# Chunk-selecting attention with a squared-ReLU way up and down: earlier first scores, the first x in pairs, the last tokens in column halves, and some squares on GpSimd

## The chip, the cores and the metric

The kernel runs on one core of one Trainium2 chip. The metric is the device time of one execution in microseconds (us). The text calls the engines by the names of the profile: PE is TensorE (matrix products), DVE is VectorE, ACT is ScalarE, POOL is GpSimd, and SP is SyncE, which here only issues DMAs.

## The reference

Two stages follow one another. The first is attention over 4 batches, 8 heads, 768 tokens and 64 columns a head, in which each token looks only at the six key chunks (of 32 keys) that an upper bound picks. The second takes the result as 3072 tokens of 512 columns through a way up to 2048 columns, a ReLU, a square, and a way down.

```python
k_chunks = k.reshape(B, H, nc, chunk, D)              # chunk = 32, nc = 24
k_min, k_max = np.min(k_chunks, axis=3), np.max(k_chunks, axis=3)
ub = np.sum(np.maximum(q[:, :, :, None, :] * k_min[:, :, None, :, :],
                       q[:, :, :, None, :] * k_max[:, :, None, :, :]), axis=-1)
ub = np.where(causal, ub, -1e9)
top_chunks = np.argsort(ub, axis=-1)[..., -6:]
scores = scale * np.matmul(q, k.transpose(0, 1, 3, 2))
mask = sel & (pos[:, None] >= pos[None, :])           # sel: the token's six chunks
attn = softmax(np.where(mask, scores, -1e9))
x = np.matmul(attn, v)                                # to [3072, 512]
h = np.maximum(x @ w_in, 0.0)
out = h * h @ w_out
```

## The kernel before

The work is cut into eight half batches of 384 tokens (`ORDER`), and each of these into four pairs of heads, so there are 32 steps s (`slots`), which the text calls pairs 0 to 31. The order of all instructions is written by hand: each engine runs its own in the order in which the program lists them, and waits at the head of its queue for what an instruction needs.

A step has these parts. `step_P` transposes k and q of a pair on PE (tiles tk and tq); ACT makes the two ReLU parts of q (`relus_T`, tile qr) and DVE the chunk extrema (`extrema`, tiles km and kbd). `step_U` multiplies them into the upper bounds (ub), from which DVE takes the sixth largest (MAX8) and writes a comparison. `step_V` transposes that comparison (qt), and DVE copies it into kq, beside the q and k that `place` puts there. `step_E` multiplies the scores (ps), ACT takes the exponential (e), and POOL masks the diagonal blocks in place (an affine select on line 416). `step_F` multiplies e with v (po), and DVE divides into x. In the text the masks, po and x are counted by the pair.

When the four pairs of a half batch are done, `step_X` transposes x to xT; for half batches 0, 1 and 7 this runs on PE with a copy on DVE and one on ACT, for the others as a DMA. `ffn_up` is one of 16 column groups f of the way up: four products (ph), the ReLU on ACT (ht, line 491), and the square on DVE (h, line 493). `ffn_down` is one quarter of the way down for 128 tokens (py, line 503); after the fourth quarter the result is copied (ob) and stored. Both lie in a queue of pieces (`queue`), from which `f1` takes one at a time at chosen places of the next half batch's steps, so the way up of half batch 0 runs in pairs 4 to 7, four groups a pair, and its way down begins with pair 8.

The first two pairs' q and k come as float32 through SP's and ACT's queues (`load_staged`) and are cast (`step_cast`). Everything else is loaded by POOL's queue, at places that `at` and `go` give by the step. `busy(n)` multiplies n blocks of an identity into a tile that nobody reads. `blank` zeroes the columns of qn0 that carry the comparison for pairs 0 to 3; three memsets zero `nsel`, which does the same for later pairs. After the last step, `step_X(7)` and the whole way up and down of half batch 7 remain.

Of the kernel before, what the change touches and what calls it, by code (L numbers as in the profile page):

```python
# [16 lines left out]
HT = 3  # L17
# [22 lines left out]
def kernel(  # L40
# [231 lines left out]

    def place(s, n, copy):
        b, half, p = slots[s]
        for h in range(2):
            copy(by_token(kqs[b % 2][QROW[h]:QROW[h] + D, h, p, 2 * half + "kq".index(n), :]),  # L276
                 in_order(st[s][n][D * h:D * h + D]))
# [171 lines left out]
    h2 = {}  # L449

    def step_X(hb, pe):
        x = xs.pop(hb)
        xT = late.tile([128, NKI, HB], BF16, tag="xT", name="xT")
        if pe:
            for g in range(2):
                pt = psA.tile([128, 2, HB], BF16, tag="att", name="pt")
                for u in range(2):
                    for j in range(HT):
                        nc.tensor.matmul(
                            pt[:, u, 128 * j:128 * (j + 1)],  # L460
                            lhsT=x[:, j, 128 * (2 * g + u):128 * (2 * g + u + 1)],
                            rhs=ident, is_transpose=True, start=True, stop=True)
                if g:
                    nc.scalar.copy(xT[:, 2:4, :], pt)
                else:
                    nc.vector.tensor_copy(xT[:, 0:2, :], pt)
        else:
            for j in range(HT):
                nc.sync.dma_start_transpose(
                    out=xT[:, :, 128 * j:128 * (j + 1)], in_=x[:, j, :])  # L470
# [4 lines left out]
        downs.extend(ffn_downs(hb, hb == 2 * B - 1))  # L475
        if hb < 2 * B - 1:
            queue.extend(downs.pop(0) for _ in range(LAG))

    def ffn_downs(hb, tail=False):
        py = {}  # L480
        return [lambda act, t=t, c=c: ffn_down(hb, py, t, c, act, tail)
                for t in range(HT) for c in range(4)]

    def ffn_up(hb, xT, f):
# [7 lines left out]
        h = late.tile([128, HB], BF16, tag="h", bufs=2 * NFI + 2, name="h")  # L492
        nc.vector.tensor_mul(h, ht, ht)  # L493
        h2[hb, f] = h
# [81 lines left out]

    def busy(n):

        idle = psA.tile([128, 128], F32, tag="att", name="idle")
# [12 lines left out]
    place(0, "k", nc.scalar.copy)  # L592
    step_U(0)
    busy(9)
    step_cast("k", 1)
    step_cast("q", 1)
    for i in range(3):
        nc.vector.memset(nsel[i], 0.0)
    step_V(0)
    step_P(1)  # L600
    step_T2(1)
    for s in range(NP):
        step_E(s, 0, 0)
        step_E(s, 0, 1)
        step_E(s, 1, 0)
        busy(8)
        step_U(s + 1)
        if s + 1 < NP:
            place(s + 1, "k", nc.scalar.copy)
        else:  # L610
            place(s + 1, "k", nc.vector.tensor_copy)
        step_E(s, 1, 1)
        if s + 1 == NP:
            place(s + 1, "q", nc.scalar.copy)
        if s:
            step_F(s - 1, 0)
            step_F(s - 1, 1)
        step_V(s + 1)
        step_P(s + 2)
        if s + 1 < NP:  # L620
            relus_T(s + 2)
            extrema(st[s + 2]["k"], s + 2)
        go(s, 99)
# [6 lines left out]
    for s, (b, half, p) in enumerate(slots):  # L630
# [16 lines left out]
        if s == NP:  # L647
# [4 lines left out]
            relus_T(s + 1)  # L652
            early.close()
            late = ctx.enter_context(tc.tile_pool(name="late", bufs=2))
            step_X(0, True)
            extrema(st[s + 1]["k"], s + 1)
            place(s + 1, "k", nc.vector.tensor_copy)
            place(s + 1, "q", nc.scalar.copy)
        if s == 2 * NP:
            for n in range(hf):  # L660
                step_E(s, 0, n)
            relus_T(s + 1)
            place(s + 1, "q", nc.scalar.copy)
            step_F(s - 1, 0)
            step_F(s - 1, 1)
            f1()
            f1()
            step_X(1, True)
            extrema(st[s + 1]["k"], s + 1)
# [12 lines left out]
        if p == 0 and hb > 2:  # L682
            f1()
            f1()
        if hb > 1:
            f1()
# [37 lines left out]
    while queue:  # L724
        fill(1, len(queue) % 2 == 0)


# [28 lines left out]
```

## Time and profile before

| | |
|---|---|
| median of 3 runs | 281.27 us (281.25 to 281.73) |
| profiled execution | 281.18 us, of it span 279.5 us |
| PE busy | 261.1 us (93% of the span) |
| DVE busy | 169.0 us (60%) |
| ACT busy | 181.1 us (65%) |
| POOL busy | 91.9 us (33%), DMA issues counted |
| mean granted clock of PE | 0.986 |
| chain that ended last | PE 70%, DVE 13%, ACT 10%, issue 3%, DMA 2% |

The span is the time from the first to the last instruction of the profiled execution; its own time has 1.7 us more around it. A busy PE is not PE at its peak, as products are pipelined and their ends modelled. The chain that ended last is followed back from the last instruction, at each step to what released it. In a timeline each line gives the start, the busy time, the engine, the line of the program, the operation, and what it writes and reads; in brackets stands how long the engine was idle before it, and what ended that.

### The profile page before, as it was taken

How to read it: one execution, taken by the hardware profiler on the slowest of the kernel's cores; microseconds unless marked ns; L12 is line 12 of the kernel's file. 1: busy time of each engine (PE TensorE's matmuls, PEld its weight loads, DVE VectorE, ACT ScalarE, POOL GpSimd, SP SyncE). 2: the span in 40 equal slices, each digit the busy share in tenths (PEclk: the TensorE clock that was granted, in tenths of full speed). 3: DMA queues.
4: the chain of work that ended last, by engine and by line, in shares of the span. 5: the costliest groups of instructions: out<-in, count | busy, mean ns of one | idle time of the engine just before them, and what ended most of it. 6: DMA issues, size and time to landing. Idle time of an engine off the chain costs nothing.

```text
span 279.5 us, 6636 instructions
## 1 busy us (share of the span) xinstructions
PE 261.1 (93%) x2463; PEld 162.3 (58%) x2463; DVE 169.0 (60%) x643; ACT 181.1 (65%) x396; POOL 91.9 (33%) x137
## 2 busy tenths in 40 slices
PE   7686989899999999999999999999999999999994
PEld 7465556546657566665565566655565566755541
DVE  6688599656896248744795368635884355413411
ACT  6595699658986578845674687835674777715500
POOL 8696336513652104731452016521111111100000
PEclk9998699999999999999999999999999999999999
DMA  8999999957999547999599359996512200101101
GB/s 144 143 211 207 179 217 193 104 68 101 166 166 162 106 96 129 137 144 159 104 143 151 77 119 153 128 138 164 135 39 55 79 2 0 40 38 39 40 38 75
DMA packets 97840, 32.05 MB, mean 115 GB/s; under 512 B 84592, under 2 KB 93424, under 8 KB 97808
## 3 DMA queue, kind: packets, MB, share of 16 engines
q0 software_dynamic: 64720, 14.42, 62.7%
q1 hardware_dynamic: 32688, 17.11, 28.1%
q8 instruction: 19, 0.31, 0.5%
q10 hardware_dynamic: 400, 0.10, 0.2%
q14 instruction: 13, 0.11, 0.1%
HBM read 27.26 MB, written 6.29 MB: 120 GB/s over the span
## 4 chain that ended last, share of the span: by engine, by line
PE 70%; DVE 13%; ACT 10%; issue 3%; DMA 2%; SPq 1%; POOL 0%; ACTq 0%; POOLq 0%
PE py L503 28%; PE ph L487 23%; PE ps L407 9%; PE po L432 6%; ACT e L412 4%; DMA stage<-in_q_dram 2%; DVE h L493 2%; ACT ht L491 2%; DVE km L319 2%; DVE x L442 2%; ACT ob L509 1%; ACT qr L271 1%; ACT kq L276 1%; PE ub L354 1%; DVE kq L276 1%
## 5 line engine op out<-in xcount | busy, mean ns | idle before, releaser
L412 ACT ACTIVATE e<-ps 128x512 bf16<-128x512 f32 x192 | 96.7, 551 | 27.2 <-PE ps L407 27.1
L487 PE MATMUL ph<-xT,w_in 128*128 128x384 bf16 x512 | 101.9, 331 | 1.3 <-ACT ht L491 0.8
L503 PE MATMUL py<-w_out,h 128*128 128x512 bf16 x384 | 92.1, 379 | 1.8 <-ACT ob L509 1.6
L491 ACT ACTIVATE ht<-ph 128x384 bf16<-128x384 f32 x128 | 62.6, 499 | 27.8 <-PE ph L487 26.0
L416 POOL TENSOR_SCALAR_AFFINE_SELECT e<-e 128x384 bf16<-128x384 bf16 x64 | 34.3, 542 | 139.7 <-ACT e L412 138.5
L493 DVE TENSOR_TENSOR h<-ht 128x384 bf16<-128x384 bf16 x128 | 46.6, 375 | 45.6 <-ACT ht L491 45.3
L487 PEld LDWEIGHTS <-w_in 128*128 128x128 bf16 x512 | 48.3, 99 | 32.3 <-issue 5.2
L407 PE MATMUL ps<-kq 128*128 128x384 bf16 (+2 forms) x320 | 56.4, 278 | 2.5 <-DVE kq L393 1.8
L503 PEld LDWEIGHTS <-h 128*128 128x128 bf16 x384 | 36.4, 98 | 37.9 <-issue 2.5
L407 PEld LDWEIGHTS <-kq 128*128 128x128 bf16 x320 | 26.5, 98 | 15.3 <-issue 3.3
L361 DVE MAX8 m<-ub 128x8 f32<-128x24 f32 (+1 forms) x160 | 16.8, 172 | 22.4 <-PE ub L354 21.5
L432 PEld LDWEIGHTS <-e 128*128 128x128 bf16 x672 | 25.5, 98 | 5.6 <-POOL e L416 1.0
L432 PE MATMUL po<-vn,e 128*128 128x65 bf16 x672 | 26.9, 194 | 0.8 <-POOL e L416 0.8
L509 ACT COPY ob<-py 128x512 f32<-128x512 f32 x19 | 11.1, 585 | 22.7 <-PE py L503 22.3
L442 DVE TENSOR_TENSOR x<-po,r 128x384 bf16<-128x384 f32 x32 | 17.8, 558 | 1.1
L393 DVE COPY kq<-qt 64x384 bf16<-64x384 bf16 (+1 forms) x28 | 8.8, 315 | 12.2 <-PE qt L389 12.2
L105 POOL DMA_DIRECT2D kn<-in_k_dram x15 | 13.3, 888 | 0.2
L105 POOL DMA_DIRECT2D qn<-in_q_dram x15 | 13.3, 886 | 0.0
L319 DVE TENSOR_TENSOR km<-km 128x384 bf16<-128x384 bf16 (+3 forms) x40 | 11.5, 287 | 1.1
L354 PE MATMUL ub<-kbd,qr 128*128 128x48 bf16 (+1 forms) x160 | 9.3, 180 | 2.3 <-DVE kbd L218 1.1
L121 POOL DMA_DIRECT2D vn<-in_v_dram x12 | 10.7, 904 | 1.8 <-DVE kq L383 1.3
L511 DVE COPY ob<-py 128x512 f32<-128x512 f32 x5 | 3.5, 691 | 11.5 <-PE py L503 11.5
(63 smaller groups left out, 194.5 us busy)
## 6 DMA issues: line engine op xcount, KB each, us to landing
out_dram<-ob SPq DMA_DIRECT2D x24, 256.0 KB, 2.1
kq<-kqT SPq DMA_DIRECT2D x10, 384.0 KB, 4.9
w_in<-in_moe_w_in_dram POOLq DMA_DIRECT2D x2, 1024.0 KB, 13.0
w_out<-in_moe_w_out_dram POOLq DMA_DIRECT2D x2, 1024.0 KB, 18.8
kn<-in_k_dram POOLq DMA_DIRECT2D x15, 128.0 KB, 5.6
qn<-in_q_dram POOLq DMA_DIRECT2D x15, 128.0 KB, 5.5
vn<-in_v_dram POOLq DMA_DIRECT2D x12, 128.0 KB, 8.0
vn<-in_v_dram POOLq DMA_DIRECT2D x4, 384.0 KB, 7.1
```

Source lines behind the costliest of these rows:

```text
L105: nc.gpsimd.dma_start(out=nat_of(n, g)[:, DM * j:DM * j + DM].rearrange("p (h d) -> p h d", d=D), in_=rows(n, *ORDER[g], 0, H)[:, 128 * j: ...
L319: nc.vector.tensor_tensor(y, x[:, :, :, 0:m], x[:, :, :, m:2 * m], op=op)
L361: nc.vector.max(out=m8[:, j, hh, :], in_=ub[:, j - j0, hh, :])
L407: nc.tensor.matmul(ps[:, at:at + 128 * m], lhsT=kqs[b % 2][:, hh, p, 2 * (j // HT), 128 * (j % HT):128 * (j % HT + 1)], rhs=qc(s, hh)[:, c ...
L412: nc.scalar.activation(e[:, 512 * n + lo:512 * n + hi], ps[:, lo:hi], ACT.Exp, scale=float(scale))
L416: nc.gpsimd.affine_select(out=d, in_=d, compare_op=ALU.is_ge, fill=0.0, base=0, channel_multiplier=-1, pattern=[[0, 3], [1, 128]])
L432: nc.tensor.matmul(po[:, hh, i, :], lhsT=t["e"][hh][:, c:c + 128], rhs=vn[b % 2][:, 2 * p + hh, j, :], start=(j == 0), stop=(j == iq))
L442: nc.vector.tensor_mul(x[:, :, 128 * p:128 * (p + 1)].rearrange("p j (h d) -> p h j d", h=2), po[:, :, :, 0:D], r.to_broadcast([128, 2, HT ...
L487: nc.tensor.matmul(ph[:, 0:HB], lhsT=w_in[:, ki, 128 * f:128 * (f + 1)], rhs=xT[:, ki, :], start=(ki == 0), stop=(ki == NKI - 1))
L491: nc.scalar.activation(ht, ph[:, 0:HB], ACT.Relu)
L493: nc.vector.tensor_mul(h, ht, ht)
L503: nc.tensor.matmul(py[t], lhsT=h2[hb, f][:, 128 * t:128 * (t + 1)], rhs=w_out[:, f, :], start=(f == 0), stop=(f == NFI - 1))
```

## The change

Five things change, and a few names with them.

1. *Start.* One half of pair 1's staged q is issued from ACT's queue. The zeroing of qn0 goes from ACT to two memsets on POOL, ahead of POOL's first loads; the zeroing of nsel goes from DVE to ACT. The first two score products and exps of pair 0 are moved ahead of the cast of pair 1's q and of pair 1's transposes.
2. *First x.* The transposes of half batch 0 are cut: those of pairs 0 and 1 come while pair 3 is worked on, that of pair 2 after po of pair 3, and that of pair 3 alone at the end; the copies are all on DVE, and the PSUM space is that of the way up. Ten and eight identity products are put between. Half of the copy of k for pair 4 goes from DVE to ACT.
3. *Second x.* The transposes of pairs 4 and 5 are moved ahead of po of pair 7; one group of the way down is moved from before the third and fourth score products of pair 8 to later in it.
4. *Squares.* Of the 16 squares of half batch 0, the eight with odd f are computed on POOL.
5. *End.* The last 128 tokens go down in two halves of 256 columns; each is copied in two parts, on DVE and ACT, and stored by two DMAs, from SP's and ACT's queues.

```diff
-    load_staged("q", 1, nc.sync, nc.sync)
+    load_staged("q", 1, nc.scalar, nc.sync)
...
     make_identity(nc, ident)
+    for c in (0, 3):
+        nc.gpsimd.memset(qn0[:, :, :, c, :], 0.0)
     load_packed("k", 0, 4)
...
-    def blank():
-        for c in (0, 3):
-            nc.scalar.mul(qn0[:, :, :, c, :].rearrange("p j a d -> p (j a) d"),
-                          ident[:, 0:D].unsqueeze(1).to_broadcast([128, HT * NP, D]), 0.0)
+    def blank(i):
+        nc.scalar.mul(nsel[i].rearrange("p j h d -> p (j h) d"),
+                      ident[:, 0:D].unsqueeze(1).to_broadcast([128, 2 * HT, D]), 0.0)
...
+    def x_T(hb, g, pt, us=(0, 1)):
+        if (hb, g) not in pts:
+            pts[hb, g] = pt[0].tile([128, 2, HB], BF16, tag=pt[1], name="pt")
+        for u in us:
+            for j in range(HT):
+                nc.tensor.matmul(
+                    pts[hb, g][:, u, 128 * j:128 * (j + 1)],
+                    lhsT=xs[hb][:, j, 128 * (2 * g + u):128 * (2 * g + u + 1)],
+                    rhs=ident, is_transpose=True, start=True, stop=True)
+    def x_copy(hb, g, u0, u1, copy):
+        copy(xT_of(hb)[:, 2 * g + u0:2 * g + u1, :], pts[hb, g][:, u0:u1, :])
...
+    def ffn_last(hb):
+        t, w = HT - 1, DM // 2
+        r0 = S * ORDER[hb][0] + HB * ORDER[hb][1] + 128 * t
+        for g in range(2):
+            y = psS.tile([128, DM], F32, tag="ps", name="py")
+            for f in range(NFI):
+                nc.tensor.matmul(
+                    y[:, 0:w], lhsT=h2[hb, f][:, 128 * t:128 * (t + 1)],
+                    rhs=w_out[:, f, w * g:w * g + w], start=(f == 0), stop=(f == NFI - 1))
+            ob = late.tile([128, DM], F32, tag="ob", bufs=3, name="ob")
+            for c in range(2):
+                (nc.scalar.copy if c else nc.vector.tensor_copy)(
+                    ob[:, 128 * c:128 * c + 128], y[:, 128 * c:128 * c + 128])
+                (nc.scalar if c else nc.sync).dma_start(
+                    out[r0:r0 + 128, w * g + 128 * c:w * g + 128 * c + 128],
+                    ob[:, 128 * c:128 * c + 128])
...
-        nc.vector.tensor_mul(h, ht, ht)
+        (nc.gpsimd if hb == 0 and f % 2 else nc.vector).tensor_mul(h, ht, ht)
...
     busy(28)
-    blank()
     step_cast("k", 0)
+    blank(1)
     step_cast("q", 0)
+    blank(2)
...
     place(0, "k", nc.scalar.copy)
+    blank(0)
     step_U(0)
     busy(9)
     step_cast("k", 1)
+    step_V(0)
+    step_E(0, 0, 0)
+    step_E(0, 0, 1)
     step_cast("q", 1)
-    for i in range(3):
-        nc.vector.memset(nsel[i], 0.0)
-    step_V(0)
     step_P(1)
     step_T2(1)
+    early.close()
+    late = ctx.enter_context(tc.tile_pool(name="late", bufs=2))
     for s in range(NP):
-        step_E(s, 0, 0)
-        step_E(s, 0, 1)
+        last = s + 1 == NP
+        if s:
+            step_E(s, 0, 0)
+            step_E(s, 0, 1)
...
+        if last:
+            x_T(0, 0, F)
         step_V(s + 1)
         step_P(s + 2)
-        if s + 1 < NP:
+        if last:
+            x_copy(0, 0, 0, 2, nc.vector.tensor_copy)
+            busy(10, *F)
+        else:
...
             relus_T(s + 1)
-            step_X(0, True)
+            x_T(0, 1, F, (0,))
+            x_copy(0, 1, 0, 1, nc.vector.tensor_copy)
+            busy(8, *A)
+            x_T(0, 1, F, (1,))
+            x_copy(0, 1, 1, 2, nc.vector.tensor_copy)
+            push(0)
...
             place(s + 1, "q", nc.scalar.copy)
+            x_T(1, 0, A)
+            x_copy(1, 0, 0, 2, nc.vector.tensor_copy)
             step_F(s - 1, 0)
             step_F(s - 1, 1)
             f1()
             f1()
-            step_X(1, True)
+            x_T(1, 1, A)
+            x_copy(1, 1, 0, 2, nc.scalar.copy)
+            push(1)
...
-        if hb > 1:
+        if hb > 1 and s != 2 * NP:
             f1()
...
     while queue:
         fill(1, len(queue) % 2 == 0)
+    ffn_last(2 * B - 1)
```

More of the change, by code (lines that the diff above doesn't have):

```diff
@@ L271, in relus_T, with place @@
             nc.scalar.activation(o, i, ACT.Relu, scale=(-1.0, 1.0)[w])
-    def place(s, n, copy):
+    def place(s, n, copy, h0=0, h1=2):
         b, half, p = slots[s]
-        for h in range(2):
+        for h in range(h0, h1):
             copy(by_token(kqs[b % 2][QROW[h]:QROW[h] + D, h, p, 2 * half + "kq".index(n), :]),
@@ L481, in ffn_downs @@
         return [lambda act, t=t, c=c: ffn_down(hb, py, t, c, act, tail)
-                for t in range(HT) for c in range(4)]
+                for t in range(HT - tail) for c in range(4)]
+    def ffn_last(hb):
[14 more added lines that the diff above has]
+                    ob[:, 128 * c:128 * c + 128])
     def ffn_up(hb, xT, f):
```

45 lines of the change are left out of this document (22 added, 23 removed).

## The prediction

> **What bounds the kernel now.** The views were read in this order: the slices of the page, for where TensorE's clock falls; a table of windows, for how busy TensorE was around that; the chain of waits, for what ends last in the first 63 us; then the timelines of GpSimd (POOL), TensorE (PE) and ScalarE (ACT) where the change cuts in.
>
> ```profile
> PEclk9998699999999999999999999999999999999999
> ```
>
> ```profile
> 9.07:12.49 3.42, 1.97 (x27) 1.53 (x28) 1.45 (x8) 2.50 (x7) 3.42 (x5) 1.00 1.78 102
> ...
> 22.73:26.14 3.41, 2.00 (x38) 1.55 (x38) 2.70 (x9) 1.51 (x4) 2.41 (x4) 1.00 1.12 208
> 26.14:29.56 3.42, 2.62 (x13) 1.48 (x13) 3.22 (x7) 2.49 (x7) 0.64 (x1) 0.50 1.26 200
> 29.56:32.97 3.41, 3.41 (x17) 1.72 (x16) 1.58 (x8) 1.58 (x4) 0.62 (x1) 0.50 2.09 169
> ```
>
> ```profile
> 63.00:243.30 180.30, 176.37 (x1689) 111.16 (x1688) 111.36 (x443) 125.53 (x273) 55.01 (x79) 1.00 0.93 112
> ```
>
> The columns of a window are its length, the busy time of PE, weight loads, DVE, ACT and POOL, then the granted clock. Behind 63 us PE is busy for 176.37 of 180.30, so a shift is only passed on. From 26.14 to 32.97 the clock is 0.50, right behind a window in which PE was busy for only 2.00 us. That is where the first x is turned and the way up begins:
>
> ```profile
> 2.77 6.69 DMA stage<-in_q_dram
> ...
> 24.29 0.56 DVE x L442
> ...
> 26.73 0.84 PE pt L459 x6
> ...
> 27.59 0.81 ACT xT L464
> ...
> 55.14 1.74 PE py L503 x8
> ```
>
> ```profile
> 26.73 0.82 PE L459 MATMUL pt<-ident,x 128*128 128x128 bf16 x6 [0.55 <-DVE x L442]
> 29.40 0.49 ACT L491 ACTIVATE ht<-ph 128x384 bf16<-128x384 f32 x1
> 37.31 0.54 PE L432 MATMUL po<-vn,e 128*128 128x65 bf16 x12
> 42.21 0.50 ACT L491 ACTIVATE ht<-ph 128x384 bf16<-128x384 f32 x1
> ```
>
> The first ht comes at 29.40, 2.67 us behind the last turning of x: half clock, and a copy of 0.81 on ACT that all four column blocks wait for. POOL is not on this chain, but its queue runs in order, and the change puts work into it:
>
> ```profile
> 1.08 0.29 POOL masks.py:199 TENSOR_SCALAR_AFFINE_SELECT ident<-ident 128x128 bf16<-128x128 bf16 x1
> 33.09 0.90 POOL L532 DMA_DIRECT2D w_out<-in_moe_w_out_dram  x1 [0.64 <-DMA vn<-in_v_dram]
> 34.00 1.22 POOL L416 TENSOR_SCALAR_AFFINE_SELECT e<-e 128x384 bf16<-128x384 bf16 x2
> 40.91 1.78 POOL L121 DMA_DIRECT2D vn<-in_v_dram  x2 [0.47 <-issue]
> 43.12 0.53 POOL L416 TENSOR_SCALAR_AFFINE_SELECT e<-e 128x384 bf16<-128x384 bf16 x1 [0.43 <-ACT e L412]
> 43.61 0.88 POOL L121 DMA_DIRECT2D vn<-in_v_dram  x1
> 45.50 0.52 POOL L416 TENSOR_SCALAR_AFFINE_SELECT e<-e 128x384 bf16<-128x384 bf16 x1 [1.01 <-ACT qr L271]
> 46.01 1.75 POOL L105 DMA_DIRECT2D kn<-in_k_dram  x2
> 48.59 0.52 POOL L416 TENSOR_SCALAR_AFFINE_SELECT e<-e 128x384 bf16<-128x384 bf16 x1 [0.82 <-ACT e L412]
> 49.05 0.88 POOL L105 DMA_DIRECT2D kn<-in_k_dram  x1
> 50.72 0.54 POOL L416 TENSOR_SCALAR_AFFINE_SELECT e<-e 128x384 bf16<-128x384 bf16 x1 [0.79 <-ACT e L412]
> ```
>
> These are the masks (L416) that every po product waits for, and DMA issues, each holding POOL for 0.88 us. Here POOL still waits for work; the last mask before po of pair 7 ends at 51.26.
>
> **Part by part.** *Head.* The chain goes through the wait for the staged q of pair 1 (6.69 us, to 9.46).
>
> ```profile
> 8.30 0.49 DVE L383 COPY kq<-qt 128x768 bf16<-128x768 bf16 x1
> 9.53 0.51 ACT L233 CAST qn<-stage 128x384 bf16<-128x384 f32 x1 [2.30 <-DMA stage<-in_q_dram]
> 11.13 1.26 ACT e L412 x3
> ```
>
> The change issues one half of that q from ACT's queue, drops three memsets from DVE (so the copy at 8.30 runs at about 8.0), and puts two score products and their two exps ahead of the cast. Copy to 8.5, product 0.4, two exps of 1.26/3 = 0.42 on average: ACT reaches the cast at about 9.75 instead of 9.53, now held by its own exps and not by the DMA. So the second selection comes 0.2 later, while ACT has two exps fewer behind it. The two memsets on POOL (6 x 128 columns; masks.py's memset of 128 columns and the select above, 0.2 to 0.3, bound them at 0.6 to 1.7 us each, I take 0.75) push POOL's loads back by 1.5, which can hold pair 2's q or the first po for up to 0.7. Nothing is paid for the zeroing that moves to ACT, or for the copy of pair 4's k, half of which moves from DVE to ACT: ACT waits there (2.30 in the row above). I price the head at +0.3 (bounds -0.3 and +1.0) at pair 4. It costs nothing in the end, because of the cover named next.
>
> *First x by pairs.* Ten and eight idle products fill the two holes of PE before 26.7, the first two pairs are turned earlier, the last two one by one, and the 0.81 copy leaves ACT for DVE in two narrow pieces. With the clock at 1.00 the last piece is copied at about 27.3 and the first ht comes at 27.7 instead of 29.40: 1.7 sooner. Groups of four ph products, 1.30 at half clock, then cost 0.65. So PE is ready for po of pair 4 near 34.7 instead of 37.31. It cannot run then. Its masks stand on POOL behind the issue of w_out at 33.09, which waits for a load of vn to land; that landing follows the DMA engines' backlog, not PE, and I leave it at 33.3. Issue 0.90, mask 0.54, one square, mask 0.54: with a square of 0.90 the second mask ends at 36.2 and po at 36.5. That is 1.35 before 37.85, and it hides up to 1.5 us of trouble in the head, the whole clock saving included. If that cover went (an earlier landing), the head's +0.3 would count.
>
> *Squares on GpSimd.* Eight leave DVE:
>
> ```profile
> L493 DVE TENSOR_TENSOR h<-ht 128x384 bf16<-128x384 bf16 x128 | 46.6, 375 | 45.6 <-ACT ht L491 45.3
> ```
>
> 8 x 0.375 = 3.0 us of DVE, which gains little, as ACT has no shorter pair than before. No row shows a product on POOL. From below: the select of the same shape, 0.54. From above: 1.1, three times the DVE row. Value taken: the selects of 128 and 384 columns give (0.54 - 0.29)/256 = 0.98 ns a column and 0.17 fixed; two inputs at twice that slope give 0.92, so 0.9. [...]
>
> The square of f = 9 stands ahead of the vn issues and waits for its ht. In the rows above that ht ends at 42.71, 4.86 behind po of pair 4 (37.85); with po at 36.5 it ends at 41.4. From there POOL has no gap: issues 1.78 + 0.88 + 1.75 + 0.88 = 5.29, masks 0.53 + 0.52 + 0.52 + 0.54 = 2.11, four squares 3.6. The mask of pair 7 ends at 52.4 instead of 51.26. PE, which would come to it at 50.7 (51.73 in a row below, less 1.0 of the 1.35), stands still for 1.7 us, and everything of PE queued behind it (eight py products, the second x, the next scores) waits too.
>
> *Second x, one way-down group fewer.*
>
> ```profile
> 51.73 0.54 PE L432 MATMUL po<-vn,e 128*128 128x65 bf16 x12
> 52.10 1.89 PE L503 MATMUL py<-w_out,h 128*128 128x512 bf16 x8
> ...
> 54.64 0.49 PE L459 MATMUL pt<-ident,x 128*128 128x128 bf16 x6 [0.32 <-ACT kq L276]
> ...
> 57.54 1.02 PE L503 MATMUL py<-w_out,h 128*128 128x512 bf16 x4 [0.67 <-ACT ob L509]
> ```
>
> py starts at 52.65 instead of 52.10: +0.55. Behind it, 53.83 to 55.14 was spent on both turnings of x and a wait; the first now lies inside the stall, so 1.31 - 0.49 = 0.82 goes. The wait of 0.67 for the output copy goes too, as scores are put between. Sum: +0.55 - 0.82 - 0.67 = -0.95. ACT then gets its next q placed a group of py sooner, which removes this wait:
>
> ```profile
> 65.51 0.81 PE L487 MATMUL ph<-xT,w_in 128*128 128x384 bf16 x4 [0.45 <-ACT ht L491]
> ```
>
> -0.45. From 67 us on PE is the bound, so both are kept.
>
> *Tail.*
>
> ```profile
> 265.36 10.37 PE py L503 x48
> 275.74 0.02 issue
> 275.76 0.69 DVE ob L511
> ```
>
> ```profile
> out_dram<-ob SPq DMA_DIRECT2D x24, 256.0 KB, 2.1
> ```
>
> 32 products of 256 columns replace 16 of 512: 10.37/48 = 0.216 each, half that and a little more for the start, 3.5 in all, +0.05. The copy of 0.69 becomes two of 128 columns side by side, about 0.3: -0.4 (bounds -0.5 and 0). A quarter of the data in the last transfer, which lands 2.1 after issue: -0.1 (0 to -0.5). Sum -0.45.
>
> All: -0.95 - 0.45 - 0.45 = -1.85. The profiled execution took 281.18 us (span 279.5 and 1.7 around it), so 279.3; the median of the runs, 281.27, lies 0.1 above it: 279.4. About 0.2% (0.56 us) is what a measurement of this kernel tells from no change.
>
> **Rivals.** *1: the POOL stall halves the clock.* One mechanism: if the mask of pair 7 ends after 53.2, PE does almost nothing from 50.7 until then, and a stretch like 22.73 to 26.14 (2.00 busy, then 0.50 for 6.83 us) comes back in a place where PE is the bound. The point is a square of 1.06 us, since each 0.1 moves that end by 0.5. For it: POOL has no slack there. Against: 9.07 to 12.49 was no busier (1.97) and kept the clock. [...] Price: start of py 1.4 later than before instead of 0.55, so a sum of -1.0; 6.83 us at half clock lose 3.4, of which PE was the bound for some 0.8: +2.8. Time 283.1. *2: POOL is quick.* With a square at 0.54 or less po of pair 7 runs at 50.7 and the stall of 1.7 goes: 277.7. For it: the select of that size. Against: it reads one input. *3: given back.* A square of 1.1, the clock kept, and ACT no sooner at 65.5: -1.85 + 1.0 + 0.45 = -0.4, time 280.9. For it: two inputs at twice the select's slope are a guess of 0.9, and the product may cost its upper bound. Against: 65.5 then waits for nothing new. *That the change does not do what it says:* the idles miss the window and 26 to 33 stays at half clock. Then po of pair 4 comes 0.3 later, as POOL holds it anyway: 279.7, within the first case.
>
> **Numbers.** Forecast 0.52 (279.4; its own range 278.6 to 280.4, squares of 0.75 to 1.05 and the tail's bounds). Rival 1: 0.21. Rival 2: 0.13. Rival 3: 0.14. The range 277.7 to 283.2 leaves out half of rival 2 and somewhat under half of rival 1. Faster: 0.52 + 0.13 and a third of rival 3, 0.69; within 0.2%: 0.09 of rival 3; slower: rival 1 and a little, 0.22.
>
> **What would show it.** Clock 1.00 from 26 to 33; first ht near 27.7; po of pair 4 near 36.2, released by POOL; POOL without gaps from 41.4 to 52.4 and a PE wait of about 1.7 us for POOL before po of pair 7; no wait of py for ob near 57; one mean for the new product on POOL near 0.9. A square under 0.6, or po of pair 7 not released by POOL, makes it wrong on the low side; a second stretch at 0.50 near 53 to 60, on the high side.

## The result: slower, by 0.94% in six runs and by 0.38% in twelve

| | median us | runs from to | ratio to before, 95% interval |
|---|---|---|---|
| before (beside the first six) | 280.87 | 279.66 to 281.73 | |
| changed kernel, first six runs | 283.55 | 283.28 to 283.85 | 1.0094, [1.0069, 1.0118] |
| changed kernel again, twelve runs on another occasion | 281.64 | 279.77 to 283.70 | 1.0038, [1.0010, 1.0067] |
| forecast | 279.4 | 277.7 to 283.2 | |

The ratio is the record's estimate from the fast runs of both kernels and not the quotient of the medians; the median of before beside the twelve was 280.23 us. The forecast had the wrong sign. The profiled execution of the changed kernel took 283.49 us (span 281.8).

**Clock.** First the slices of the page, then a table of windows of the changed kernel (length; busy time of PE, weight loads, DVE, ACT, POOL; granted clock).

```profile
PEclk9999999889999999999999999999999999999999
```

```profile
17.24:20.65 3.41, 3.41 (x44) 3.01 (x43) 1.88 (x10) 2.51 (x6) 2.74 (x5) 1.00 1.00 193
...
51.37:54.78 3.41, 1.75 (x30) 1.36 (x31) 1.04 (x3) 2.83 (x7) 3.40 (x6) 1.00 1.42 87
54.78:58.20 3.42, 3.20 (x14) 1.22 (x12) 2.98 (x7) 0.10 (x1) 1.90 (x3) 0.50 1.32 84
```

In this execution the half clock that stood at 26 to 33 is gone. A new stretch stands at 54.78 to 58.20, behind a window in which PE was busy for 1.75 us and POOL for 3.40. A third stretch doesn't show in these rows: up to 20.65 the trace has no record of the clock, and both views print that as full speed. The products tell it. TensorE's timeline of the changed kernel, then of before:

```profile
1.43 3.17 PE L617 MATMUL idle<-ident 128*128 128x128 bf16 x28 [1.43 <-POOL ident masks.py:199]
5.50 0.54 PE L251 MATMUL tk<-ident,kn 96*64 96x96 bf16 x8 [0.91 <-DVE kn L232]
...
12.89 1.06 PE L617 MATMUL idle<-ident 128*128 128x128 bf16 x8
```

```profile
4.53 0.54 PE L250 MATMUL tk<-ident,kn 96*64 96x96 bf16 x8
...
6.52 0.66 PE L581 MATMUL idle<-ident 128*128 128x128 bf16 x9
```

Before, nine idle products took 0.66 at 6.5 us; in the changed kernel eight take 1.06 at 12.9. From one idle product's start to the next it is 0.107 us up to there and 0.056 later, in both traces. So the changed kernel ran at half clock for 20.65 us, before for 5.66. And TensorE begins pair 0 at 5.50 instead of 4.53, with a hole of 0.91 in front, which leads to VectorE.

**The head.** The timelines of POOL, DVE and ACT of the changed kernel; under them DVE of before.

```profile
1.31 1.41 POOL L150 MEMSET qn<- 128x768 bf16 x2
...
1.40 1.73 DVE L159 TENSOR_SCALAR oneh<-ident 64x768 bf16<-64x768 bf16 x1
...
5.02 0.42 DVE L232 CAST kn<-stage 96x512 bf16<-96x512 f32 x1
...
10.84 0.87 ACT L413 ACTIVATE e<-ps 128x512 bf16<-128x512 f32 x2 [2.25 <-PE ps L408]
11.60 0.51 ACT L234 CAST qn<-stage 128x384 bf16<-128x384 f32 x1
```

```profile
1.40 0.55 DVE L156 TENSOR_SCALAR oneh<-ident 64x768 bf16<-64x768 bf16 x1
...
3.90 0.42 DVE L231 CAST kn<-stage 96x512 bf16<-96x512 f32 x1
```

The two memsets are as short as priced (0.74 each), but VectorE's oneh, 0.55 alone, starts beside them and ends 0.41 after they do: 1.73. The cast of k follows 1.1 later, and the cast of q of pair 1, now queued behind two exps, starts at 11.60 instead of 9.53.

**The stall.** The chain of waits of the changed kernel:

```profile
43.25 0.39 ACT ht L527
43.64 0.07 issue
43.71 0.83 POOL h L529
44.54 0.37 POOL vn L121
...
52.33 0.79 POOL h L529
53.12 0.08 POOL kn L105
53.20 0.79 issue
53.99 0.55 POOL e L417
54.54 0.05 issue
54.58 0.39 PE po L433 x6
54.97 0.43 PE py L539
55.40 0.22 issue
55.62 2.74 PE py L539 x6
```

From the ht of f = 9 on, every step up to po of pair 7 is POOL's. The "issue" pieces in between are inside POOL's DMA issues. TensorE's timeline there:

```profile
53.22 0.35 PE L433 MATMUL po<-vn,e 128*128 128x65 bf16 x6 [0.65 <-DVE xT L473]
54.58 0.39 PE L433 MATMUL po<-vn,e 128*128 128x65 bf16 x6 [1.01 <-POOL e L417]
```

PE waits 0.65 for VectorE's copy of the turned x, does half of po, and waits 1.01 for POOL's mask. Behind it eight py products (seven are on record) take 3.39 up to the next turning, at half clock; before they took 1.73.

Milestones of all the kernels, read as starts of rows on the timelines (us; the last column is the ratio of the timed runs):

| kernel | first po | po pair 4 | first py | next tokens' ph | span | ratio |
|---|---|---|---|---|---|---|
| before | 14.99 | 37.31 | 52.10 | 63.16 | 279.5 | |
| changed | 18.54 | 38.23 | 54.78 | 66.12 | 281.8 | 1.0094 |
| e5 changed again | 17.09 | 36.71 | 53.38 | 64.58 | 280.0 | 1.0038 |
| e1 squares on VectorE | 18.51 | 38.29 | 54.22 | 63.87 | 280.1 | 0.9984 |
| e2 zeroing on ScalarE | 14.86 | 35.22 | 52.47 | 62.12 | 277.8 | 0.9953 |
| e3 both | 15.06 | 34.69 | 51.77 | 61.42 | 277.0 | 0.9922 |
| e4 before, squares on GpSimd | 14.85 | 35.47 | 52.30 | 64.55 | 280.9 | 1.0052 |
| e6 before, zeroing on GpSimd | 14.81 | 36.70 | 51.54 | 62.59 | 278.7 | 0.9983 |
| e7 37 first idles | 15.84 | 35.03 | 52.10 | 63.06 | 279.5 | 1.0046 |
| e8 e3 without idles at first x | 14.87 | 34.13 | 50.43 | 60.08 | 275.6 | 0.9928 |
| e9 old start order | 14.81 | 35.49 | 52.95 | 62.61 | 278.4 | 0.9988 |
| e10 e8, other tile for second x | 17.15 | 36.14 | 52.05 | 61.71 | 278.0 | 0.9920 |
| e11 four early squares only | 18.11 | 37.55 | 53.44 | 63.09 | 279.9 | 1.0016 |
| e12 e8, first x in one piece | 16.05 | 35.43 | 52.46 | 62.12 | 277.9 | 0.9950 |
| e13 stall filled | 18.53 | 38.31 | 54.86 | 64.52 | 280.9 | 1.0021 |
| e14 e8, filled head | 15.12 | 34.47 | 51.37 | 61.03 | 276.5 | 0.9947 |
| e15 before, filled first x | 15.30 | 35.44 | 50.37 | 61.43 | 277.7 | 0.9971 |
| e16 changed, filled head | 16.49 | 35.67 | 53.17 | 62.82 | 278.7 | 1.0037 |

The column of pair 4 is the start of its first po product. In e2, e3, e8, e9, e10, e12 and e14 PE stops inside this po for 0.24 to 0.95 us, until a load of v has landed, and goes on between 34.76 (e8) and 37.19 (e10). In e3 that load was issued at 19.55:

```profile
34.69 0.56 PE L436 MATMUL po<-vn,e 128*128 128x65 bf16 x5
36.10 0.38 PE L436 MATMUL po<-vn,e 128*128 128x65 bf16 x7 [0.86 <-DMA vn<-in_v_dram]
```

So a head that is in time runs into this landing, and what it gains there is partly lost.

A span is one execution, and executions of one kernel differ by 2 to 4 us (first and third row of the first table; the last section has what goes with it). So a row tells a mechanism, and the ratio what it is worth; each ratio is known to about 0.003 to either side.

### The profile page after: what moved, and what is told of

Its sections match the earlier page's. It is cut to its first block, busy times and chain, and to the rows that moved or that the text cites. A ratio compares the mean times of both kernels' runs of the same rounds, so it can differ in the third digit from the quotient of the medians.

```text
span 281.8 us, 6692 instructions
## 1 busy us (share of the span) xinstructions
PE 263.7 (94%) x2472; PEld 168.4 (60%) x2497; DVE 168.0 (60%) x634; ACT 181.1 (64%) x399; POOL 99.8 (35%) x147
## 4 chain that ended last, share of the span: by engine, by line
PE 75%; ACT 8%; DVE 8%; issue 4%; POOL 3%; DMA 1%; ACTq 0%; POOLq 0%
PE py L539 27%; PE ph L523 23%; PE ps L408 10%; PE po L433 7%; ACT e L413 3%; ACT ht L527 2%; PE idle L617 2%; DVE km L320 1%; ACT ob L545 1%; POOL e L417 1%; POOL h L529 1%; PE ub L355 1%; ACT kq L277 1%; PE qt L390 1%; DVE h L529 1%
## 5 line engine op out<-in xcount | busy, mean ns | idle before, releaser
L523 PE MATMUL ph<-xT,w_in 128*128 128x384 bf16 x512 | 99.2, 326 | 1.3 <-ACT ht L527 1.0
L539 PE MATMUL py<-w_out,h 128*128 128x512 bf16 x343 | 85.5, 384 | 2.8 <-ACT ob L545 0.9
L529 DVE TENSOR_TENSOR h<-ht 128x384 bf16<-128x384 bf16 x120 | 44.1, 378 | 43.2 <-ACT ht L527 42.9
L523 PEld LDWEIGHTS <-w_in 128*128 128x128 bf16 x512 | 47.5, 97 | 30.8 <-issue 2.6
L408 PE MATMUL ps<-kq 128*128 128x384 bf16 (+2 forms) x320 | 57.6, 283 | 1.5 <-DVE kq L384 0.9
L539 PEld LDWEIGHTS <-h 128*128 128x128 bf16 x368 | 35.3, 99 | 36.2 <-issue 3.4
L617 PE MATMUL idle<-ident 128*128 128x128 bf16 x97 | 10.2, 280 | 1.4 <-POOL ident masks.py:199 1.4
L272 ACT ACTIVATE qr<-tq 128x256 bf16<-128x256 bf16 (+1 forms) x24 | 8.8, 428 | 4.0 <-PE tq L244 3.9
```

The source lines that it names most:

```text
L408: nc.tensor.matmul(ps[:, at:at + 128 * m], lhsT=kqs[b % 2][:, hh, p, 2 * (j // HT), 128 * (j % HT):128 * (j % HT + 1)], rhs=qc(s, hh)[:, c ...
L523: nc.tensor.matmul(ph[:, 0:HB], lhsT=w_in[:, ki, 128 * f:128 * (f + 1)], rhs=xT[:, ki, :], start=(ki == 0), stop=(ki == NKI - 1))
L529: (nc.gpsimd if hb == 0 and f % 2 else nc.vector).tensor_mul(h, ht, ht)
L539: nc.tensor.matmul(py[t], lhsT=h2[hb, f][:, 128 * t:128 * (t + 1)], rhs=w_out[:, f, :], start=(f == 0), stop=(f == NFI - 1))
```

## The experiments

The theory: the zeroing on GpSimd makes the head late and cold, the squares on GpSimd make the mask of pair 7 late, and the clock falls behind that. The rivals: the clock falls by itself, wherever its windows happen to lie; or the other parts of the change bring nothing.

**e1, all squares on VectorE.**

```diff
-        (nc.gpsimd if hb == 0 and f % 2 else nc.vector).tensor_mul(h, ht, ht)
+        nc.vector.tensor_mul(h, ht, ht)
```

> The changed kernel with all sixteen squares of the first half on VectorE; nothing else differs. Theory (the zeroing costs the head, the squares make GpSimd late for the masks of pair 7): the stall before po of pair 7 (about 2 us, up to 54.6) goes, and with it the half clock of 54.78 to 58.20, while the first 20 us stay at half clock: 280.6 us (280.0 to 281.3). Rival (PE is late there only because the head is late, and the clock falls by itself): 282.8 or more, with a second stretch at half clock.

280.34 us, ratio 0.9984, [0.9957, 1.0012]. The clock was full from 20.58 us to the end, as the theory had it, and py to the next ph took 9.65 instead of 11.34. But py started only 0.56 sooner: in place of the stall stands a chain of VectorE, from before 46 without a gap to a copy of kq that ends at 52.13 and holds the next scores up to 52.27, and behind these the wait for its copy of the turned x (0.65, up to 53.85).

**e2, zeroing on ScalarE.**

```diff
-    for c in (0, 3):
-        nc.gpsimd.memset(qn0[:, :, :, c, :], 0.0)
...
+    blank_q()
     step_cast("k", 0)
-    blank(1)
     step_cast("q", 0)
-    blank(2)
...
-    blank(0)
+    for i in (1, 2, 0):
+        blank(i)
```

`blank_q` holds the two `nc.scalar.mul` of the kernel before.

> The changed kernel with qn zeroed on ScalarE ahead of the casts, as in the kernel before, instead of by two memsets on GpSimd; the three blankings of nsel go behind the placing of pair 0's k. Theory: oneh takes 0.55 again instead of 1.73, the cast of k comes near 4.0 instead of 5.02, PE has no hole behind its first 28 idle products, the clock is full from about 6 us, and the copy of kq of pair 3 comes near 20.5 instead of 23.58; the stall before pair 7 stays, about 1 us sooner: 282.2 us (281.6 to 282.8). Rival (the clock's late rise has nothing to do with the hole): half clock up to about 20 us and 283.5 as before.

279.63 us, ratio 0.9953, [0.9927, 0.9980]: already faster than before, by more than expected. The timeline of VectorE:

```profile
1.40 0.55 DVE L157 TENSOR_SCALAR oneh<-ident 64x768 bf16<-64x768 bf16 x1
...
3.91 0.42 DVE L235 CAST kn<-stage 96x512 bf16<-96x512 f32 x1
```

The clock was full from 5.26 us, and the second cast of q started at 9.76 (the prediction had 9.75). po of pair 7 still waited for GpSimd, whose mask ended at 52.20, and the clock held behind it.

**e3, both.** The two edits together.

> Both of these edits together: squares on VectorE and qn zeroed on ScalarE, the rest of the change kept. Theory: the gains of the first x, the second x and the tail come out: 278.9 us (278.2 to 279.6), clock full from about 6 us to the end. Rival (these parts bring nothing): 280.9, the time of the kernel before, or more.

278.90 us, ratio 0.9922, [0.9895, 0.9950], as the theory had it. What is left of the change is worth 2.2 us of the 281.01 measured beside it.

**e4, the squares alone, in the kernel before.** The line of e1 the other way round.

> The kernel before with every second square of the first half on GpSimd, the rest as it was. Theory: from the ht of f = 9 at 42.7 GpSimd works without a gap, 5.29 of issues, 2.11 of masks and 4 squares of 0.83, so the mask of pair 7 ends near 53.4 instead of 51.26; py starts 1.5 to 2 us later than 52.10, and the clock is lost behind that: 282.8 us (281.6 to 284.0; 282.0 if the clock holds). Rival (GpSimd keeps up, and VectorE is relieved): 280.9 or less.

282.63 us, ratio 1.0052, [1.0024, 1.0080]. The mask of pair 7 ended at 52.04 instead of 51.27, though po of pair 4 ran 1.84 sooner in this execution, and the clock fell from 52.72 to 56.14: py to the next ph took 12.25 instead of 11.06. The squares cost by themselves: from the end of po of pair 4 to py it took 16.0 us instead of 14.25.

**e5, the changed kernel again**, because these four don't add up to 283.55.

> The changed kernel itself, unaltered, beside the three that follow and on the chip that they share. What was measured so far does not add up: taking the zeroing away and taking the squares away gave 278.90, and either alone 279.63 and 280.34, which by adding would make the changed kernel 281.1 instead of 283.55. Theory (the stretches in which the clock is granted lie differently from run to run against the kernel's start, and the first six runs had the worst place): the runs spread over some 3 us and the median is 281.0 to 282.5. Rival (the two costs are worth more together than apart, whatever the place): 283.3 to 283.9 again, in a narrow band.

281.64 us, ratio 1.0038, [1.0010, 1.0067], runs over 3.9 us: the theory. One of these twelve took as long as the first six; why all of the first six did is not shown. In this execution the clock rose at 5.32, and then:

```profile
8.74:12.15 3.41, 1.81 (x29) 1.27 (x26) 1.90 (x5) 1.74 (x5) 2.88 (x4) 1.00 1.47 94
12.15:15.56 3.41, 2.99 (x30) 1.97 (x28) 2.03 (x8) 2.52 (x7) 2.19 (x5) 0.50 1.39 137
...
49.69:53.11 3.42, 1.67 (x26) 1.28 (x27) 1.21 (x4) 2.83 (x8) 3.41 (x6) 1.00 2.62 129
53.11:56.52 3.41, 3.19 (x13) 1.47 (x15) 2.80 (x7) 0.26 (x1) 2.06 (x3) 0.50 2.26 111
```

Against this run, e2 takes 0.0085 off and e1 0.0054, and e3, with both, 0.0116: within the intervals they add.

**e6, the zeroing alone, in the kernel before**: the two memsets ahead of GpSimd's loads, and no blanking on ScalarE.

> The kernel before with qn zeroed by two memsets on GpSimd ahead of its loads, in place of the two blankings on ScalarE; the rest as it was. Theory (the memset holds up VectorE's oneh, PE waits behind its first idle products, and the clock rises late): oneh 1.73 instead of 0.55, the cast of k near 5.0, a hole of 0.9 on PE, half clock to about 20 us in some of the runs: 282.0 us (281.5 to 283.0). Rival (the head's lateness is hidden by the wait for GpSimd's masks at pair 4, as the prediction had it): 281.0.

279.91 us, ratio 0.9983, [0.9962, 1.0004]: no loss, as the rival had it, but not by its reason. oneh took as long and the hole was there (0.90), yet the first po came at 14.81, so nothing was left to hide at pair 4: the cast of q ran at 8.05, with no exps ahead of it. The staged q, too, was there sooner: with POOL's loads issued 1.1 us later it landed 3.7 us after its issue (median of three) instead of 6.6. In this order the zeroing does not cost.

**e7, the hole filled**: 37 first idle products instead of 28.

> The changed kernel with 37 first idle products instead of 28, so that PE works up to about 5.6 us, when the cast of k is done. Theory (the hole is what keeps the clock down): the clock is full from 7 us at the latest, kq of pair 3 is copied near 21 instead of 23.58, and the median is about 1.4 below that of the unaltered changed kernel. Rival (VectorE's 1.1 us are the cost, or other stretches are too empty as well): half clock to about 20 us as before and the same time as the changed kernel within 0.3.

281.56 us, ratio 1.0046, [1.0022, 1.0070]: no gain over 1.0038. The clock rose at 6.96, and in this execution the first po came 1.25 sooner than in e5; the runs as a whole did not gain. Filling the hole brings nothing that these runs can tell.

**e8, e3 without the ten and eight idle products at the first x.**

> The version with squares on VectorE and qn zeroed on ScalarE, without the 18 idle products (ten and eight) around the first turnings of x; everything else of the change stays. Theory (the idles keep the clock there, as the prediction had it): half clock again behind 24 to 26 us in most runs, first ht about 1 us later, 280.3 us (279.7 to 281.0). Rival (spreading the turnings keeps the clock without them): 278.9, as with them, or a little less.

278.43 us, ratio 0.9928, [0.9903, 0.9954]: the rival. In the trace the clock held from 4.96 up to the stores without them.

**e9, the order of the start as before**, with zeroing and squares left on GpSimd.

```diff
+    step_cast("q", 1)
     step_V(0)
-    step_E(0, 0, 0)
-    step_E(0, 0, 1)
-    step_cast("q", 1)
     step_P(1)
...
-        if s:
-            step_E(s, 0, 0)
-            step_E(s, 0, 1)
+        step_E(s, 0, 0)
+        step_E(s, 0, 1)
```

> The changed kernel with the order of the start as before: the cast of q of pair 1 comes ahead of the first scores and their exps again. Zeroing and squares stay on GpSimd. Theory (the zeroing's 1.1 us on VectorE reach the path only because the exps, which wait for VectorE's kq, now stand ahead of that cast on ScalarE; in the old order they hide behind the wait for the staged q): the second cast near 8 to 9.5 instead of 10.7 to 11.6, first po near 15 instead of 17.1 to 18.5, and a ratio to the kernel before of 0.995 (0.993 to 0.998) instead of 1.004. Rival (the zeroing costs in any order): 1.004.

280.52 us, ratio 0.9988, [0.9956, 1.0019]. The cast started at 8.48 and the first po came at 14.81, as the theory had it, though the cast no longer waited for the staged q (as in e6); of the 0.0085 that e2 gained, 0.0050 came back, less than expected. The two ratios are each known to about 0.003, so this is just clear of noise. With e6 it makes the zeroing's price one of order: the 1.1 us of VectorE reach the path through the two exps that the change put ahead of the cast.

**e10, e8 with the second x turned into ph's buffer.**

```diff
-            x_T(1, 0, A)
+            x_T(1, 0, F)
```

> The fastest version so far (squares on VectorE, zeroing on ScalarE, no idles at the first x), with the first turning of the second x written to the accumulator buffer of ph instead of the one that po takes next. Theory (po of pair 7 waits for VectorE to copy the turned x out of the buffer it needs): po of pair 7 0.6 sooner, a ratio 0.002 below that version's, 0.991 (0.989 to 0.993). Rival (po waits for other work of VectorE anyway): 0.993.

278.45 us, ratio 0.9920, [0.9889, 0.9951]: too close to e8's to tell the two apart. The trace does tell. The timeline of TensorE of e3, whose turning has the old buffer, and then of e10:

```profile
50.25 0.50 PE L470 MATMUL pt<-ident,x 128*128 128x128 bf16 x6
51.40 0.53 PE L436 MATMUL po<-vn,e 128*128 128x65 bf16 x12 [0.65 <-DVE xT L476]
```

```profile
51.34 0.50 PE L470 MATMUL pt<-ident,x 128*128 128x128 bf16 x6
51.67 0.54 PE L436 MATMUL po<-vn,e 128*128 128x65 bf16 x12
```

The wait for VectorE's copy of x is gone, and from the end of po of pair 4 to py it took 14.48 us instead of 15.3 in e3 and e8.

**e11, only f = 1, 3, 5, 7 on GpSimd** (`f % 2 and f < 8` in the line of e1).

> The changed kernel with only the squares of f = 1, 3, 5 and 7 on GpSimd, those of f = 9 to 15 on VectorE. Theory (only the late four stand in the gapless chain before the mask of pair 7): no wait of PE for GpSimd before po of pair 7, ratio as with no square on GpSimd, 0.998 (0.996 to 1.001). Rival (the early ones cost as well, ahead of the masks of pairs 4 and 5): 1.002 or more.

281.30 us, ratio 1.0016, [0.9984, 1.0048]. po of pair 7 no longer waited for GpSimd (its mask ended at 51.46, po ran at 53.07) and py to the next ph took 9.65. Whether the early four cost something of their own stays open: the interval holds both expectations.

**e12, e8 with the first x turned in one piece behind po of pair 3**, as before.

> The fastest version so far, with the first x turned as in the kernel before: both halves behind po of pair 3, copied by VectorE and ScalarE. Theory (turning by pairs, and not the idles, shortens the way to the first ht and keeps the window of the clock filled): half clock again behind 23 to 26 us in most runs, first ht 1 to 2 us later, ratio 0.998 (0.996 to 1.000) instead of 0.993. Rival (the gain at the first x comes from elsewhere, such as the freer VectorE and ScalarE of the head): 0.993.

279.61 us, ratio 0.9950, [0.9922, 0.9977], between the two; by the runs alone it is not told from e8. In the trace it took 3.77 from po of pair 3 to the first ht (25.62 to 29.39) instead of 2.86 (24.37 to 27.23 in e8), but the clock held there, and 7 of the 12 runs have a mean granted clock of 0.998 or more. So the pairs shorten the way, and are not needed to keep the clock.

**e13, 16 idle products in the stall** of the changed kernel.

```diff
             x_copy(1, 0, 0, 2, nc.vector.tensor_copy)
+            busy(16, *F)
             step_F(s - 1, 0)
```

> The changed kernel with 16 idle products in the stall before po of pair 7, which change no result and no order. Theory (the stall costs twice: by itself, and because the clock halves behind a window with so little work): GpSimd's mask comes as late as before, py starts as late, but the clock stays full from 50 to 60, py to the first ph of the next tokens takes 9.7 us instead of 11.2, and the ratio is 0.999 to 1.001 instead of 1.004. Rival (the stall alone is the price): 1.004.

280.82 us, ratio 1.0021, [0.9990, 1.0052]; the interval holds both. In the trace the step is as expected: the mask as late as before, and then full clock.

```profile
52.49 1.06 PE L617 MATMUL idle<-ident 128*128 128x128 bf16 x16
53.38 0.35 PE L433 MATMUL po<-vn,e 128*128 128x65 bf16 x6
54.66 0.36 PE L433 MATMUL po<-vn,e 128*128 128x65 bf16 x6 [0.93 <-POOL e L417]
54.86 1.89 PE L539 MATMUL py<-w_out,h 128*128 128x512 bf16 x8
```

py to the next ph took 9.66. In the unaltered kernel it took 11.34 and 11.20: the clock's share of the stall is 1.6 us where the window falls so. The runs as a whole do not show this gain.

**e14 and e16, a filled head**: `busy(6)` behind step_V(0) and ahead of step_P(1), in e8 and in the changed kernel.

> The fastest version (squares on VectorE, zeroing on ScalarE, no idles at the first x) with six idle products behind pair 0's turned selection and six ahead of pair 1's turnings, where TensorE waits. Theory (the runs differ by whether a window between 6 and 12 us falls under some 37% of the array's capacity): no half clock after its first rise, the slower half of the runs disappears, median ratio 0.990 (0.988 to 0.992). Rival (the idles lengthen the head as much as they save): 0.993.

> The changed kernel with the same twelve idle products in its head; zeroing and squares stay on GpSimd. Theory (of what the zeroing costs, part is VectorE's 1.1 us on the path, and part the clock that stays or falls to half up to 20 us): first po near 16 instead of 17.1 to 18.5, ratio 1.000 (0.998 to 1.002). Rival (filling holes does not bring the clock, or the 1.1 us are all): 1.004.

278.36 us, 0.9947, [0.9914, 0.9981], and 282.62 us, 1.0037, [1.0000, 1.0074]: neither gained, and e14 spread wider than e8 (277.28 to 280.97 against 277.24 to 279.10). In e16's trace the clock fell all the same, from 7.62 to 11.03, where an idle product takes 0.107 us instead of 0.056. Both theories fell, and the times are those of the rivals.

**e15, ten and eight idle products at the first x, in the kernel before.**

> The kernel before with ten and eight idle products at the first turnings of x, and nothing else. This is the prediction's first step by itself: the clock at 26 to 33. Theory (the fill keeps the clock and the time reaches py, since po of pair 4 is not in truth held by GpSimd at a fixed time): clock full from 26 to 33, first ht 1 us sooner, po of pair 4 near 36, ratio 0.995 to 0.998. Rival, the prediction's own step (GpSimd's masks hold po of pair 4 to 36.5 or later and hide most of it): 0.999 to 1.000.

279.74 us, ratio 0.9971, [0.9945, 0.9996]. The clock was full from 5.77 up to the stores and po of pair 4 ran at 35.44 instead of 37.31; nearly all of it reached py (50.37 instead of 52.10). The first ht did not come sooner (29.39 against 29.40), as po of pair 3 ran 0.31 later here: what the clock gives comes behind it. With all squares on VectorE, GpSimd's two masks there ended at 34.88, so they held nothing.

## Why the prediction was wrong

The forecast against three executions, in four stretches (us; the forecast's are its own terms, put on the rows of before; the others are read from the rows):

| | forecast | changed, first | e5 | e2 |
|---|---|---|---|---|
| end of po of pair 4 | 36.5 | 38.77 | 37.25 | 36.46 |
| from there to the first py | 16.15 | 16.01 | 16.13 | 16.01 |
| from py to the next tokens' ph | 9.57 | 11.34 | 11.20 | 9.65 |
| from there to the end of the span | 215.4 | 215.7 | 215.4 | 215.7 |
| span | 277.6 | 281.8 | 280.0 | 277.8 |

Two steps failed. The head was priced at +0.3 and thought covered: at the end of po of pair 4 the kernel is 2.27 behind the forecast in the first execution and 0.75 in e5. And the forecast let the clock stay full behind the stall, leaving its fall to rival 1: 1.77 and 1.63. Together they make nearly all of the difference. With the zeroing undone (e2), in an execution whose clock held, all four stretches come out within 0.3; over its runs e2 gained 0.0047, or 1.3 us.

- **Head, +0.3 (bounds -0.3 and +1.0): this step failed.** Measured to the first po: +3.55 in the profiled execution, +2.10 in e5, -0.13 in e2. The price of the memsets was right (0.74 for 0.75). Left out was VectorE beside them, which the prediction let run 0.3 sooner: oneh took 1.73 with the memsets on GpSimd (also in e1) and 0.55 without them (before, e2, e3 and e4). And the new order on ScalarE passes VectorE's lateness on to the cast of q. Not all of the lateness is the order's: e7 came +0.85 with a clock that was full from 6.96 on, and e10, with the zeroing on ScalarE, came +2.16 with half clock from 10.39 to 17.22. So the larger part of +3.55 and +2.10 is half clock in the head, which the prediction did not price. Whether the late head makes the clock fall there more often is not shown.
- **The cover of 1.5 us: wrong in size.** It rested on the issue of w_out at 33.3 whatever TensorE does; that the landing before it follows the DMA engines' backlog alone was the author's reading of before, where the loads of v issued up to 19.9 took 4.7 to 15.5 to land. Measured: 34.73 in the profiled execution, 33.22 in e5, 32.95 in e2. In e9, whose head is in time, GpSimd did release the second half of po there at 36.58 (forecast: second mask ends 36.2), for a wait of 0.34. In e2 that half started at 36.08, almost as forecast, but by luck: the load of v released it, and the masks had ended before. Against a head that is 3.5 late the cover hid nothing: po of pair 4 ended 0.92 later than before, instead of 1.35 sooner.
- **First x, 1.7 sooner at the first ht: 1.23 of it, and wrong in its reason.** From po of pair 3 to ht: 2.86 in the profiled execution (28.58 to 31.44) and 2.85 in e5, against 4.09 before. With full clock and x in one piece it takes 3.77 (e12, e15), so the pairs give 0.91 here and the clock 0.32. The clock's price comes behind ht: from there to po of pair 4 it took 7.91 before and 6.05 in e15. The idle products are not what keeps the clock in the changed kernel, as e8 and e12 show; what in the rest of the change does is open. The loss that the prediction saw is the kernel's and not only that execution's: of the 126 runs of before that the ratios of e1 to e16 rest on, 87 have a mean granted clock under 0.990 (the profiled one has 0.986) and 9 have 0.998 or more, and the two other traces that keep its first x unfilled (e4, e6) lost the clock between 23 and 30 as well. But its place and length vary, and e15, which fills it, gained 0.0029, or 0.8 us.
- **Squares at 0.9 (bounds 0.54 and 1.1): right, 0.836.** The row:

```profile
L529 POOL TENSOR_TENSOR h<-ht 128x384 bf16<-128x384 bf16 x8 | 6.7, 836 | 7.9 <-ACT ht L527 7.8
```

  GpSimd ran without a gap from ht of f = 9 to the mask of pair 7 but for 0.17 at 49.2, in 10.9 us (43.64 to 54.54) where 11.0 had been summed. So the stall came as described, up to 54.54 instead of 52.4 because ht of f = 9 was late with the head. PE waited 1.01 for POOL there and not 1.7, as 0.65 of it now goes to VectorE's copy of the turned x, which the prediction put at nothing.
- **Rival 1, the clock halves behind that stall: it happened**, in the profiled execution, e5, e7 and e4, not in e2 and e9. Its point, a mask later than 53.2, does not decide: in e7 it ended at 51.72 and the clock fell, in e9 at 52.69 and it held. How the stall lies to the windows agrees with the count in the last section (34% before the fall in the profiled execution), but was not tested. Its time, 283.1, was near the first result by luck: the late head, which the rival did not have, made part of that.
- **Second x, -0.82 - 0.67 - 0.45: right behind py, with a price ahead of it.** py to the next ph took 9.65 wherever the clock held, against 11.06: -1.41 for -1.49. The turning gave its 0.81 (53.83 to 54.97 before, 53.50 to 53.83 in e3). The rest gave 0.60: the scores now fill the wait for the output copy, though the next py still starts only when that copy is done (56.35 and 56.39 in e3). The wait of 0.45 went too: from that ph to po of pair 8 it took 3.85 instead of 4.45. With no stall to hide it, turning x ahead of po of pair 7 costs 0.34 and the wait of 0.65 shown under e10: from the end of po of pair 4 to py e3 took 15.29 and before 14.25. In the changed kernel the stall hid it.
- **Tail, -0.45: mis-sized, about -0.15.** The 32 narrow products took +0.05, as forecast (10.73 from the last ph to the end of the last product against 10.68). From there to the end 3.56 instead of 3.74. The two copies do not run side by side: in both halves ACT's starts 0.03 to 0.04 behind the end of DVE's. The profile puts the second start down to a transfer, which landed at the same time.

```profile
276.50 0.29 DVE L514 COPY ob<-py 128x128 f32<-128x128 f32 x1 [1.05 <-PE py L509]
276.82 0.27 ACT L514 COPY ob<-py 128x128 f32<-128x128 f32 x1 [8.49 <-DVE ob L514]
278.24 0.29 DVE L514 COPY ob<-py 128x128 f32<-128x128 f32 x1 [1.46 <-PE py L509]
278.57 0.27 ACT L514 COPY ob<-py 128x128 f32<-128x128 f32 x1 [1.48 <-DMA out_dram<-ob]
```

The forecast of -1.85 us is near what the change gives without its two GpSimd parts (e3: -0.78%, [-1.05%, -0.50%], or 2.2 us). The fastest versions, e8 and e10, beat both kernels: 0.9928 [0.9903, 0.9954] and 0.9920 [0.9889, 0.9951]. The 0.2% that the prediction took for what a measurement can tell came from three runs that lay close together; the 126 runs of before lie between 278.47 and 282.94.

## What to carry to other kernels

Work given to GpSimd because it has time is priced by what stands behind it in its queue (in e4 it took 16.0 us instead of 14.25 from po of pair 4 to py) and by what VectorE does at that moment (oneh, 1.73 instead of 0.55), not by its own duration alone. When a step becomes late, follow the order of every engine that waits for it: the same lateness on VectorE cost about 1.4 us more in one order on ScalarE than in another (1.0038 against 0.9988, each known to 0.003). The place and length of a half-clock stretch in one profile belong to that execution (the changed kernel's first lasted to 20.65 in one and to 5.32 in the next); look at the spread of the runs and their granted clocks before counting the whole of it as a gain.

## What the runs showed of the hardware

- **The clock's changes lie multiples of 3.41 us apart, at places that differ from trace to trace.** Every change of it in the 18 traces lies a multiple of 3.413 us from the others of its trace, to 0.03 us (20.65, 54.78 and 58.20 in the changed kernel), with another offset in each; a window here is the 3.413 us between two such places. The spread of the runs goes with it: the 9 of the 126 runs of before with a mean granted clock of 0.998 or more have a median of 279.45 us, the 24 under 0.985 one of 281.69.
- **How full a window was before half and before full clock.** Counted in the traces: the columns of every product that ran in a window, weighted by the share of the 128 x 128 array that it filled, over what the array streams in 3.41 us at full clock (512 columns in 0.216 us, as py does). Up to its first record of the clock a trace counts as half clock, as the spacing of the idle products (0.107 us instead of 0.056) has it. Of the 378 whole windows up to 75 us, all 28 under 36% were followed by half clock, all 328 over 40% by full clock; of the 22 between, 12 by full. In the changed kernel the window up to 54.78 held 34%, and of those up to 20.65, where the clock rose, the last held 44% and the four before it 31 to 37%; in before the one up to 26.14 held 36%. Counted without the turnings it doesn't separate them: a window of 16% kept the clock, one of 33% lost it. So in this count turnings belong in, by the area that they fill: the best single limit misplaces 3 windows counted so, 14 with the area left out, and 22 without the turnings. This is a reading of traces, not a test. e13's 16 products filled 25% of the window that kept its clock, but without them it would still have held 40%. e14 and e16 were meant to use this count and gained nothing; in e16 a window of 32% (4.21 to 7.62) remained, and the clock fell behind it.
- **With half of the squares on GpSimd, VectorE's own took longer.** Between 28 and 60 us the squares on VectorE took 0.351 each before. With the other half on GpSimd they took 0.40 to 0.54 (0.404 in the changed kernel, 0.440 in e5); the most is e2's:

```profile
L493 DVE TENSOR_TENSOR h<-ht 128x384 bf16<-128x384 bf16 x16 | 5.5, 351 | 2.8 <-ACT ht L491 2.6
```

```profile
L532 DVE TENSOR_TENSOR h<-ht 128x384 bf16<-128x384 bf16 x8 | 4.3, 541 | 0.2 <-ACT ht L530 0.2
```

In e2 eight of them went, and 1.2 us of VectorE's time was saved instead of half of 5.5.
